# Loading q four tokens to a row, in the order in which the transposes write it, in a fused retention and bilinear feed-forward kernel

## The chip, the cores and the metric

The kernel runs on one core of a Trainium2 chip. The metric is the time of one execution on the device, in microseconds; the median of three runs counts. The traces come from the chip's own profiler.

## The reference

For 8 batches, 8 heads, 576 tokens and a head dimension of 64, a retention layer without softmax is computed, and its result goes through a bilinear feed-forward layer:

```python
scores = scale * np.matmul(q, k.transpose(0, 1, 3, 2))        # scale = 1/sqrt(64)
gamma = 1.0 - 2.0 ** (-5.0 - np.arange(H))                     # one decay a head
rel = pos[:, None] - pos[None, :]
Dmat = np.where(rel >= 0, gamma[:, None, None] ** rel[None], 0.0)
ret = np.matmul(scores * Dmat, v)                              # (8, 8, 576, 64)
x = ret.transpose(0, 2, 1, 3).reshape(4608, 512)
a, b = x @ w_a, x @ w_b                                        # 512 -> 1536
out = (a * b) @ w_out                                          # 1536 -> 512, float32
```

q, k, v and the weights are float32 in DRAM.

## The kernel before

All matrix products are in bfloat16 with float32 sums. The decay is split: values are scaled by gamma^-token, outputs by scale times gamma^token (the table `qs_o` in the opening), and between them stands a plain triangular mask. Tokens are handled in pairs of 128 rows (256 tokens); what lies more than a block back comes in through a running state (keys times values, summed).

**The opening.** The first 256 tokens of batches 0, 1 and 2 are handled in six steps, `STEPS = [(0, 0), (1, 0), (0, 1), (1, 1), (2, 0), (2, 1)]`: batch and half of the heads. Steps 0 to 3 (batches 0 and 1) are done before the feed-forward layer starts; steps 4 and 5 (batch 2) are done inside its first block. Here two tokens stand in a row: partition p holds tokens 2p and 2p+1, so that `load_step` (L152 to L163) moves pieces of 2 x 64 floats, 512 B, one DMA of 256 KB for each of q, k and v of a step. All go out on SP's queue, but K of step 0 on ACT's. Per step there are:

- `cast_step`: float32 to bfloat16, heads regrouped by token parity, one for q and one for k (DVE, POOL or ACT); `values_step`: the scaled values, in two parts
- `transpose_step`: four 128 x 128 transposes on TensorE for q and four for k, into one PSUM tile `tp`, and copies from there to `qkT` (L338)
- `score_step`: sixteen small products into `sc` (two PSUM banks, one tile for all steps) and the mask product on DVE into `sT` (L360)
- `state_step` and its parts: products of keys and values (L379), and copies of the state by ACT
- `open_step`, `step_states`, `step_keys`, `close_step`: output products from states (L449) and scores (L465), scaled on DVE into `xT` (L481, L486)

`warm` (L923) puts products of ones in between, whose results nobody reads. The order of the opening is written out by hand (L929 to L998): the order of the calls is the order on every engine's queue. `load_w` puts the weight loads, which turn float32 into bfloat16 on the way, on POOL's queue between casts; `load_wo` follows. After the opening, `gate`, a tiny copy out of `wo_sb`, holds SP's queue until the first piece of `w_out` has landed; behind it stand the loads of steps 4 and 5 and of the following pairs.

**The feed-forward layer.** It runs in blocks of 512 or 256 tokens: products `pa` (L860, in the first block partly L811 through `ffn_begin` and `begin_with`) and `pb` (L875), their product on DVE into `hT`, then `po` (L822 in the first block, else L896) and its copy to `osb`. The list `todo` holds the attention work that goes in between, each entry with a place in units of one 512-wide product: `early_casts` at 100, a q cast at 112.1, `third_turn` at 124, `third_states` at 128 and `third_outputs` at 136 are those of batch 2. The rest of the batches goes in pairs of 128 rows with one token a row (`load_pair`, `ahead`, `turn`, `stretch`), transposed by DMA instead of TensorE. `store` writes 128 rows of `osb`; for the first 256 tokens of batches 0 to 2 (`n < FIRST`) in two DMAs, one for each token parity. Stores of the first three blocks are held in `held` and sent from places in `todo`.

Four PSUM banks (`ps_ffn`, tag `ab`) rotate among `tp`, `w`, state products and the layer's products.

Of the kernel before, what the change touches and what calls it, by code (L numbers as in the profile page):

```python
# [10 lines left out]
FP32 = mybir.dt.float32  # L11
BF16 = mybir.dt.bfloat16
INT32 = mybir.dt.int32
# [5 lines left out]
def kernel(  # L19
# [10 lines left out]
    nc = tc.nc  # L30
# [123 lines left out]
    def load_step(n, hh, which, on=nc.sync):  # L154

        if n not in paired:
            paired[n] = [stage.tile([128, 2 * DM], FP32, tag=name, name=name)
                         for name in ("qf", "kf", "vf")]
        on.dma_start(
            paired[n][which][:, hh * DM:(hh + 1) * DM]  # L160
            .rearrange("p (h e) -> p h e", h=4),
            (q, k, v)[which][n, 4 * hh:4 * hh + 4, 0:256, :]
            .rearrange("h (p two) d -> p h (two d)", two=2))  # L163

    STEPS = [(0, 0), (1, 0), (0, 1), (1, 1), (2, 0), (2, 1)]
    Q, K, V = 0, 1, 2
    for i, which in ((0, Q), (0, K), (0, V), (2, Q), (2, K), (1, K),
                     (1, Q), (2, V), (3, K), (3, Q), (1, V), (3, V)):
        load_step(*STEPS[i], which,
                  nc.scalar if (i, which) == (0, K) else nc.sync)  # L170

# [1 line left out]

    idxp_i = const.tile([128, 2], INT32)
    nc.gpsimd.iota(idxp_i, pattern=[[1, 2]], base=0, channel_multiplier=2)
    idx_o = sum_pool.tile([128, 2, 2, 64], INT32, tag="sums", name="idx_o")
    nc.gpsimd.iota(idx_o, pattern=[[128, 2], [1, 2], [2, 64]], base=0,
                   channel_multiplier=0)
    identity = const.tile([128, 128], BF16)
    make_identity(nc, identity)  # L180
    mask_s = const.tile([128, 2, 2, 64], BF16)
    nc.gpsimd.memset(mask_s, 1.0)
    for a in (0, 1):
        nc.gpsimd.affine_select(
            out=mask_s[64 * a:64 * a + 64], in_=mask_s[64 * a:64 * a + 64],
            compare_op=ALU.is_ge, fill=0.0, base=0,
            pattern=[[-1, 2], [1, 2], [2, 64]], channel_multiplier=-2)
    idxv_i = const.tile([128, 3, 2], INT32)
    mask3 = const.tile([128, 64], BF16)

# [104 lines left out]

    QUADS = [(0, 0), (1, 1), (0, 1), (1, 0)]

    def place_step(i):
# [3 lines left out]
        transposed[key] = half_of(qkt_pool, i, [2, DM], BF16, "qkT")  # L302

    def given(i, which):
# [7 lines left out]
    COPY = {"dve": nc.vector.tensor_copy, "pool": nc.gpsimd.tensor_copy,  # L312
            "act": nc.scalar.copy}

    def cast_step(i, w, on):
        COPY[on](by_parity(natural[STEPS[i]][0][:, w]), given(i, w))  # L316

    def values_step(i, kp, on):
        n, hh = STEPS[i]
# [9 lines left out]
    def transpose_step(i, *ways):  # L329
        qkb, qkT = natural[STEPS[i]][0], transposed[STEPS[i]]  # L330
        tp = ps_ffn.tile([128, len(ways), 4, 128], BF16, tag="ab", name="tp")
        for to, (w, on) in enumerate(ways):
            for c in range(4):
                nc.tensor.transpose(tp[:, to, c, :],  # L334
                                    qkb[:, w, c * 128:c * 128 + 128],
                                    identity)
        for to, (w, on) in enumerate(ways):
            COPY[on](qkT[:, w], tp[:, to].rearrange("p c x -> p (c x)"))  # L338

    def queries(key, r, j, a):  # L340
        return transposed[key][r, 0].rearrange(
            "p (k j s) -> p j k s", k=2, j=2)[:, j, :, half(a)]

    def score_step(i, place=None, tag="sc"):
        key = STEPS[i]
# [54 lines left out]
        else:  # L400
            rest.append(keep)

    def last_states():

        own, later_half = kvs = [
            ps_ffn.tile([128, 2, 2, 64], FP32, tag="ab", name=f"kv1{a}")
            for a in (0, 1)]
        fresh = set(QUADS)
        for i in (1, 3):
            state_products(i, [kv[:, i // 2] for kv in kvs], fresh)  # L410
        for r in (0, 1):
            nc.scalar.copy(state_after[half(r), 1, :, half(r)],
                           own[half(r)].rearrange("p i j d -> p (i j) d"))
        nc.scalar.copy(own_sums[1],
                       own.rearrange("p i j d -> p (i j) d"))
        nc.scalar.copy(second[:, 1],
                       later_half.rearrange("p i j d -> p (i j) d"))
# [115 lines left out]
                decay[:, at], op=ALU.mult)  # L533
        natural[FIRST + n, "pair"] = (qkb, vb)

    def turn(n):
# [246 lines left out]
    def store(u, cols, osb):  # L783
        n, u = place(u // 2), u % 2
        for kp, r0, m, b, s0 in rows_of(n):
            rows = out[b * S + s0:b * S + s0 + m, cols]
            if kp != u:
                continue
            if n < FIRST:
                for par in (0, 1):  # L790
                    nc.sync.dma_start(rows[par::2], osb[half(par), cols])
            else:
                nc.sync.dma_start(rows, osb[r0:r0 + m, cols])

    held = []

# [130 lines left out]
    pieces = list(zip(edges, edges[1:]))  # L927
    vector, pool_ = nc.vector, nc.gpsimd
    warm(8, 512)  # L929
    make_qs(qs_o, 0, 0, 256)  # L930
    for i in range(4):
        place_step(i)
    cast_step(0, Q, "dve")
    cast_step(0, K, "dve")
    make_qs(qs_o, 1, 0, 256)
    transpose_step(0, (Q, "act"))
    transpose_step(0, (K, "dve"))
    values_step(0, 0, nc.scalar)
    values_step(0, 1, vector)
    make_qs(qs_o, 2, 0, 256)  # L940
    cast_step(2, Q, "pool")
    warm(2, 512)
    score_step(0)
    warm(1, 512)
    state_step(0)
    transpose_step(2, (Q, "dve"))
    cast_step(2, K, "pool")
    cast_step(1, K, "pool")
    warm(2, 512)
    transpose_step(2, (K, "dve"))  # L950
    warm(2, 512)
    load_w(*pieces[0], "a")
    cast_step(1, Q, "act")
    score_step(2)
    transpose_step(1, (K, "act"))
    output_step(0)
    transpose_step(1, (Q, "act"))
    values_step(2, 1, pool_)
    values_step(2, 0, pool_)
    make_qs(qs_o, 3, 0, 256)  # L960
    load_w(*pieces[0], "b")
    load_w(*pieces[1], "a")
    warm(2, 512)
    cast_step(3, K, "dve")
    score_step(1)
    cast_step(3, Q, "act")
    rest = []
    state_step(2, rest)
    warm(2, 512)
    transpose_step(3, (Q, "act"))  # L970
    transpose_step(3, (K, "dve"))
    rest.pop()()
    open_step(2)
    step_states(2, True)
    step_keys(2, {0})
    for kp in (0, 1):
        values_step(1, kp, pool_)
    values_step(3, 0, nc.scalar)
    values_step(3, 1, pool_)
    load_w(*pieces[1], "b")  # L980
    score_step(3)
    close_step(2)
    last_states()
    for i, banks in ((1, ps_ffn), (3, ps_sc)):
        open_step(i, banks)
        step_keys(i, {0, 1})
    for i in (1, 3):
        step_states(i, False)
    for i in (1, 3):
        close_step(i)  # L990
    firsts = ps_o[0].tile([128, 2, 512], FP32, tag="o", name="pa2")
    for F in range(WCOLS[0]):
        ffn_begin(F, firsts[:, F])
    for c in (0, 1):
        for F in range(WCOLS[0]):
            begin_with(F, c, 1)
# [3 lines left out]
        load_wo(i)  # L1000
    make_masks()
    nc.sync.dma_start(gate, wo_sb[0:1, 3, 0:64])
    for i, which in ((4, Q), (4, K), (4, V), (5, Q), (5, K), (5, V)):
        load_step(*STEPS[i], which)
    load_pair(FIRST)
    load_pair(FIRST + 1, (Q,))
# [14 lines left out]
    def early_casts():  # L1021
        for i in (4, 5):
            place_step(i)
        cast_step(4, Q, "act")
        for i in (4, 5):
            cast_step(i, K, "pool")
            for kp in (0, 1):
                values_step(i, kp, pool_)

# [30 lines left out]
    todo = [(100, early_casts, ()),  # L1060
            (112.1, cast_step, (5, Q, "act")),
            (124, third_turn, ()), (128, third_states, ()),
            (136, third_outputs, ())]
    todo += [(60 + 10 * n, total_of, (n,)) for n in (0, 1)]
# [31 lines left out]
    for fn, places in ((ahead, casts), (turn, turns)):  # L1096
        todo += [(at, fn, (n,)) for n, at in places.items()]
    todo.sort(key=lambda e: e[0])

# [41 lines left out]
```

## Time and profile before

| | |
|---|---|
| median of the runs (three) | 325.33 us (325.19 to 325.6) |
| the profiled execution | 325.76 us |
| its span in the profile | 324.0 us |
| busy: TensorE, VectorE (DVE) | 318.6 us, 165.5 us |
| busy: ScalarE (ACT), GpSimd (POOL) | 130.8 us, 118.8 us |
| DMA bytes | 50.90 MB, 157 GB/s in the mean |

The profile is that of one execution. PE is TensorE, SP the queue that issues most DMAs; a line number is one of the kernel before. The chain of waits follows the execution back from its last instruction, at each step to what released it. A DMA is given with the time from its issue to its landing, the moment at which its semaphore tells the waiting engines.

### The profile page before, as it was taken

The numbers are of one execution on the slowest core, as the hardware profiler recorded it, in microseconds if no ns is written. First come the engines' busy times: TensorE is split into PE (matmuls) and PEld (weight loads), VectorE is DVE, ScalarE is ACT, GpSimd is POOL, SyncE is SP. The second block draws the span as 40 slices with busy tenths as digits, with TensorE's granted clock in tenths as the row PEclk, the third lists the DMA queues.
The fourth block names the chain that finished last, engine by engine and source line by source line (L and its number), as shares of the span: only waits on it lengthen the run. The fifth ranks groups of instructions, "written<-read, shape, count | busy, mean of one in ns | idle before, by whom it ended". The sixth has DMA issues, their size and how long they took to land.

```text
span 324.0 us, 8659 instructions
## 1 busy us (share of the span) xinstructions
PE 318.6 (98%) x3607; PEld 164.4 (51%) x3607; DVE 165.5 (51%) x296; ACT 130.8 (40%) x289; POOL 118.8 (37%) x159
## 2 busy tenths in 40 slices
PE   8899999999999999999999999999999999999996
PEld 3554457777444554444454545454545444444444
DVE  4845345665546754835374627562566256514321
ACT  6745653435435523533253324442433343313321
POOL 3990076583745375457075205450520000000000
PEclk9999999999999999999999999999999999999999
DMA  8999999999999999999999168935750510031003
GB/s 215 253 202 207 261 229 195 197 181 197 182 223 243 218 192 240 229 223 230 182 211 195 47 156 194 214 78 144 169 113 15 141 42 2 2 97 32 1 23 109
DMA packets 146487, 50.90 MB, mean 157 GB/s; under 512 B 126736, under 2 KB 141968, under 8 KB 146448
## 3 DMA queue, kind: packets, MB, share of 16 engines
q1 hardware_dynamic: 140112, 45.37, 68.2%
q0 software_dynamic: 5808, 4.72, 9.3%
q8 instruction: 28, 0.46, 0.6%
q10 hardware_dynamic: 528, 0.26, 0.3%
q14 instruction: 11, 0.09, 0.1%
HBM read 37.75 MB, written 9.44 MB: 146 GB/s over the span
## 4 chain that ended last, share of the span: by engine, by line
PE 97%; ACT 1%; DVE 1%; issue 0%; DVEq 0%
PE pb L875 29%; PE pa L860 28%; PE po L896 28%; PE w L923 2%; PE po L822 2%; PE sc L635 2%; PE o L663 1%; PE o L676 1%; PE kv L573 1%; PE tp L334 1%; PE sc L352 1%; PE pa L811 1%; PE o L465 0%; ACT qkT L338 0%; ACT vb L324 0%
## 5 line engine op out<-in xcount | busy, mean ns | idle before, releaser
L880 DVE TENSOR_TENSOR hT<-ha,pb 128x512 bf16<-128x512 bf16 (+1 forms) x120 | 75.7, 632 | 93.7 <-PE pb L875 86.2
L875 PE MATMUL pb<-xT,wb_sb 128*128 128x512 bf16 (+1 forms) x480 | 111.6, 358 | 0.1
L868 ACT CAST ha<-pa 128x512 bf16<-128x512 f32 (+1 forms) x120 | 64.8, 543 | 113.6 <-PE pa L860 110.7
L860 PE MATMUL pa<-xT,wa_sb 128*128 128x512 bf16 (+1 forms) x472 | 109.8, 357 | 0.0
L896 PE MATMUL po<-wo_sb,hT 128*128 128x512 bf16 (+2 forms) x432 | 91.8, 367 | 0.0
L875 PEld LDWEIGHTS <-wb_sb 128*128 128x128 bf16 x480 | 46.9, 98 | 46.6 <-issue 0.3
L860 PEld LDWEIGHTS <-wa_sb 128*128 128x128 bf16 x472 | 45.4, 98 | 45.1 <-issue 0.4
L896 PEld LDWEIGHTS <-hT 128*128 128x128 bf16 x432 | 40.4, 98 | 44.4
L519 POOL CAST qkb<-qf 64x1024 bf16<-64x1024 f32 x15 | 15.4, 1030 | 68.2 <-DMA qf<-in_q_dram 57.9
L530 POOL TENSOR_TENSOR vb<-vf,vs 128x1024 bf16<-128x1024 f32 (+1 forms) x17 | 28.8, 1699 | 15.4 <-DMA vf<-in_v_dram 6.4
L907 DVE COPY osb<-po 128x512 f32<-128x512 f32 (+2 forms) x16 | 10.4, 649 | 39.1 <-PE po L896 39.1
L905 ACT COPY osb<-po 128x512 f32<-128x512 f32 (+1 forms) x20 | 11.4, 572 | 46.4 <-PE po L896 46.4
L519 POOL CAST qkb<-kf 64x1024 bf16<-64x1024 f32 (+1 forms) x17 | 15.9, 933 | 12.4 <-DMA kf<-in_k_dram 12.0
L598 DVE TENSOR_TENSOR sums<-kv,sums 128x256 f32<-128x256 f32 x44 | 18.6, 423 | 2.7 <-PE kv L573 0.8
L644 DVE TENSOR_TENSOR sT<-sc,mask 128x512 bf16<-128x512 f32 x30 | 19.5, 680 | 0.0
L523 POOL CAST qkb<-kf 64x512 bf16<-64x512 f32 (+1 forms) x34 | 18.6, 573 | 1.0
L523 POOL CAST qkb<-qf 64x512 bf16<-64x512 f32 x30 | 17.6, 614 | 0.6
L602 ACT CAST states<-sums 64x512 bf16<-64x512 f32 x26 | 16.0, 617 | 0.3
L689 DVE TENSOR_TENSOR xT<-o,qs 128x512 bf16<-128x512 f32 x24 | 15.4, 680 | 1.5 <-PE o L676 1.5
L923 PE MATMUL w<-ones 128*128 128x512 bf16 x19 | 7.4, 512 | 1.5 <-DVE idxp_f L204 1.5
L316 POOL CAST qkb<-kf 128x512 bf16<-128x512 f32 x4 | 2.4, 612 | 15.8 <-DMA kf<-in_k_dram 15.8
L360 DVE TENSOR_TENSOR sT<-sc,mask_s 128x1024 bf16<-128x1024 f32 x6 | 7.2, 1219 | 1.9 <-PE sc L352 1.8
(96 smaller groups left out, 173.4 us busy)
## 6 DMA issues: line engine op xcount, KB each, us to landing
qf<-in_q_dram SPq DMA_DIRECT2D x32, 256.0 KB, 4.8
vf<-in_v_dram SPq DMA_DIRECT2D x32, 256.0 KB, 5.1
kf<-in_k_dram SPq DMA_DIRECT2D x31, 256.0 KB, 4.8
out_dram<-osb SPq DMA_DIRECT2D x25, 256.0 KB, 2.5
out_dram<-osb SPq DMA_DIRECT2D x21, 128.0 KB, 2.7
wo_sb<-in_moe_w_out_dram POOLq DMA_DIRECT2D x3, 512.0 KB, 15.9
qf<-in_q_dram SPq DMA_DIRECT2D x8, 128.0 KB, 3.2
kf<-in_k_dram SPq DMA_DIRECT2D x8, 128.0 KB, 3.3
```

The source lines that it names most:

```text
L519: nc.gpsimd.tensor_copy(qkb[0:64, w, e], t[0:64, e])
L523: nc.gpsimd.tensor_copy(to[:, :, 1 - r], fro[:, :, r])
L530: nc.gpsimd.tensor_tensor(vb[:, e].rearrange("p (h d) -> p h d", d=D), t[:, e].rearrange("p (h d) -> p h d", d=D), decay[:, at], op=ALU.mult)
L598: nc.vector.tensor_tensor(sums[:, i], own, prev, op=ALU.add)
L602: nc.scalar.copy(to(half(1 - r)), fro(half(r)))
L644: nc.vector.tensor_tensor(sT[:, on].rearrange("p c k s -> p (c k) s"), sc[:, on].rearrange("p c k s -> p (c k) s"), mask3.unsqueeze(1).to_ ...
L689: nc.vector.tensor_tensor(x_of(t0, 128).rearrange("p c (a s) -> p c a s", a=2), o[:, :, :, kp].rearrange("p a c s -> p c a s"), qs[:, :, s ...
L860: nc.tensor.matmul(pa[:, 0:n], wa_sb[:, c, fs], xT[:, c], start=(c == 0), stop=(c == NC - 1))
L868: nc.scalar.copy(ha[:, 0:n], pa[:, 0:n])
L875: nc.tensor.matmul(pb[:, 0:n], wb_sb[:, c, fs], xT[:, c], start=(c == 0), stop=(c == NC - 1))
L880: nc.vector.tensor_tensor(hT[:, F, 0:n], has[F][:, 0:n], pb[:, 0:n], op=ALU.mult)
L896: nc.tensor.matmul(po[:, 0:width], hT[:, F, u * 128:(u + 1) * 128], wo_sb[:, F, cols], start=(F == 0), stop=(F == NF - 1))
```

## The change

For the three batches of the opening, q is no longer loaded by step but by batch, in four DMAs of 128 KB. DMA `h` takes heads `h` and `h + 4` to the two halves of the partitions, and each partition holds four tokens of one head, 1,024 B in one piece. The cast goes by pairs of DMAs (`cast_queries`), four transposes then turn two such pairs of heads (`turn_queries`), and `queries` reads 32 columns from each of four tokens' blocks. Keys and values stay as they were, two tokens a row. The query tokens so stand in another order in the mask, in `qs_o`, in `xT` and in the output rows, and `store` writes its 128 rows in one DMA whose DRAM side is walked as four groups of 32 rows.

The opening's order is written anew: other engines for several casts, copies and values (both value parts of step 0 on POOL, one part of step 3 on DVE), q of a batch turned at once, the kept state copies later, each `tp` tile holding four transposes rather than up to eight, two fillers fewer, and the first products of the layer (`ffn_begin`) ahead of the last products from the states instead of behind them.

```diff
@@ load_step
+        if which == Q:
+            for h in range(4):
+                on.dma_start(
+                    paired[n][Q][:, 256 * h:256 * h + 256],
+                    q[n, h::4, 0:256, :]
+                    .rearrange("g (p four) d -> g p (four d)", four=4))
+            return
@@ order of the loads
-    for i, which in ((0, Q), (0, K), (0, V), (2, Q), (2, K), (1, K),
-                     (1, Q), (2, V), (3, K), (3, Q), (1, V), (3, V)):
+    for i, which in ((0, Q), (0, K), (0, V), (2, K), (1, Q), (1, K),
+                     (2, V), (3, K), (1, V), (3, V)):
@@ casts, turns, queries
+    def cast_queries(n, j, on):
+        COPY[on](heads_q[n][:, j].rearrange("p (k h d) -> p h k d", h=2, k=4),
+                 paired[n][Q][:, j * DM:(j + 1) * DM]
+                 .rearrange("p (h k d) -> p h k d", h=2, k=4))
+    def turn(blocks, to, on):
+        tp = ps_ffn.tile([128, 4, 128], BF16, tag="ab", name="tp")
+        for c in range(4):
+            nc.tensor.transpose(tp[:, c, :], blocks[:, c * 128:c * 128 + 128],
+                                identity)
+        COPY[on](to, tp.rearrange("p c x -> p (c x)"))
+    def turn_queries(n, on):
+        for j in (0, 1):
+            turn(heads_q[n][:, j], turned_q[n][:, j], on[j])
     def queries(key, r, j, a):
-        return transposed[key][r, 0].rearrange(
-            "p (k j s) -> p j k s", k=2, j=2)[:, j, :, half(a)]
+        n, hh = key
+        p0 = 64 * hh + 32 * a
+        return turned_q[n][r, j].rearrange(
+            "p (k x) -> p k x", k=4)[:, :, p0:p0 + 32]
@@ store
             if n < FIRST:
-                for par in (0, 1):
-                    nc.sync.dma_start(rows[par::2], osb[half(par), cols])
-            else:
-                nc.sync.dma_start(rows, osb[r0:r0 + m, cols])
+                rows = rows.rearrange("(s k) m -> k s m", k=4)
+            nc.sync.dma_start(rows, osb[r0:r0 + m, cols])
@@ the opening, as it now stands
     warm(8, 512)
     for c in range(3):
         make_qs(qs_o, c, 0, 256)
     ...
     cast_keys(0, "dve")
     cast_queries(0, 0, "dve")
     cast_queries(0, 1, "act")
     turn_keys(0, "dve")
     turn_queries(0, ("act", "dve"))
     values_step(0, 0, pool_)
     values_step(0, 1, pool_)
     make_qs(qs_o, 3, 0, 256)
     cast_keys(2, "pool")
     warm(2, 512)
     score_step(0)
     warm(1, 512)
     state_step(0, keeps)
     turn_keys(2, "act")
     cast_queries(1, 0, "pool")
     load_w(*pieces[0], "a")
     cast_queries(1, 1, "act")
     warm(2, 512)
     score_step(2)
     keeps.pop()()
     cast_keys(1, "pool")
     open_step(0)
     step_states(0, True)
     step_keys(0, {0})
     warm(2, 512)
     turn_queries(1, ("act", "act"))
     turn_keys(1, "dve")
     close_step(0)
     values_step(2, 0, pool_)
     values_step(2, 1, pool_)
     load_w(*pieces[0], "b")
     warm(2, 512)
     score_step(1)
     cast_keys(3, "act")
     state_step(2, keeps)
     turn_keys(3, "act")
     open_step(2)
     step_states(2, True)
     step_keys(2, {0})
     values_step(1, 0, pool_)
     load_w(*pieces[1], "a")
     values_step(1, 1, nc.scalar)
     keeps.pop()()
     values_step(3, 0, vector)
     values_step(3, 1, pool_)
     load_w(*pieces[1], "b")
     score_step(3)
     close_step(2)
     ...
     for i, banks in ((1, ps_ffn), (3, ps_sc)):
         state_products(i, [kv[:, i // 2] for kv in kvs], fresh)
         open_step(i, banks)
         step_keys(i, {0, 1})
     last_copies(kvs)
     ...
     for F in range(WCOLS[0]):
         ffn_begin(F, firsts[:, F])
     for i in (1, 3):
         step_states(i, False)
     for i in (1, 3):
         close_step(i)
@@ batch 2, inside the first block
-    for i, which in ((4, Q), (4, K), (4, V), (5, Q), (5, K), (5, V)):
+    for i, which in ((4, Q), (4, K), (4, V), (5, K), (5, V)):
         load_step(*STEPS[i], which)
     def third_turn():
+        turn_queries(2, ("act", "act"))
         for i in (4, 5):
-            transpose_step(i, (Q, "act"), (K, "dve"))
+            turn_keys(i, "dve")
```

More of the change, by code (lines that the diff above doesn't have):

```diff
@@ L175 @@
     nc.gpsimd.iota(idxp_i, pattern=[[1, 2]], base=0, channel_multiplier=2)
-    idx_o = sum_pool.tile([128, 2, 2, 64], INT32, tag="sums", name="idx_o")
-    nc.gpsimd.iota(idx_o, pattern=[[128, 2], [1, 2], [2, 64]], base=0,
+    idx_o = sum_pool.tile([128, 2, 4, 32], INT32, tag="sums", name="idx_o")
+    nc.gpsimd.iota(idx_o, pattern=[[128, 2], [1, 4], [4, 32]], base=0,
                    channel_multiplier=0)
@@ L180 @@
     make_identity(nc, identity)
-    mask_s = const.tile([128, 2, 2, 64], BF16)
+    mask_s = const.tile([128, 2, 4, 32], BF16)
     nc.gpsimd.memset(mask_s, 1.0)
@@ L186 @@
             compare_op=ALU.is_ge, fill=0.0, base=0,
-            pattern=[[-1, 2], [1, 2], [2, 64]], channel_multiplier=-2)
+            pattern=[[-1, 2], [1, 4], [4, 32]], channel_multiplier=-2)
     idxv_i = const.tile([128, 3, 2], INT32)
@@ L296 @@
     QUADS = [(0, 0), (1, 1), (0, 1), (1, 0)]
+    heads_q, turned_q = {}, {}
     def place_step(i):
@@ L302, in place_step @@
         transposed[key] = half_of(qkt_pool, i, [2, DM], BF16, "qkT")
+        if i % 2 == 0:
+            heads_q[i // 2] = shared["qkb"][:, :, Q]
+            turned_q[i // 2] = shared["qkT"][:, :, Q]
     def given(i, which):
@@ L313, with cast_keys @@
             "act": nc.scalar.copy}
-    def cast_step(i, w, on):
-        COPY[on](by_parity(natural[STEPS[i]][0][:, w]), given(i, w))
+    def cast_keys(i, on):
+        COPY[on](by_parity(natural[STEPS[i]][0][:, K]), given(i, K))
+    def cast_queries(n, j, on):
+        COPY[on](heads_q[n][:, j].rearrange("p (k h d) -> p h k d", h=2, k=4),
+                 paired[n][Q][:, j * DM:(j + 1) * DM]
+                 .rearrange("p (h k d) -> p h k d", h=2, k=4))
     def values_step(i, kp, on):
@@ L327, in values_step, with turn_keys @@
                              .to_broadcast([128, 4, D]), op=ALU.mult)
[L329 to L338, printed above, removed]
+    def turn(blocks, to, on):
[4 more added lines that the diff above has]
+        COPY[on](to, tp.rearrange("p c x -> p (c x)"))
+    def turn_keys(i, on):
+        turn(natural[STEPS[i]][0][:, K], transposed[STEPS[i]][:, K], on)
+    def turn_queries(n, on):
+        for j in (0, 1):
+            turn(heads_q[n][:, j], turned_q[n][:, j], on[j])
     def queries(key, r, j, a):
-        return transposed[key][r, 0].rearrange(
-            "p (k j s) -> p j k s", k=2, j=2)[:, j, :, half(a)]
+        n, hh = key
+        p0 = 64 * hh + 32 * a
+        return turned_q[n][r, j].rearrange(
+            "p (k x) -> p k x", k=4)[:, :, p0:p0 + 32]
     def score_step(i, place=None, tag="sc"):
@@ L401, in state_copies, with last_copies @@
             rest.append(keep)
[L403 to L410, printed above, removed]
+    def last_copies(kvs):
+        own, later_half = kvs
         for r in (0, 1):
@@ L534, in ahead, with turn_pair @@
         natural[FIRST + n, "pair"] = (qkb, vb)
-    def turn(n):
+    def turn_pair(n):
         qkb = of(natural, n)[0]
@@ L929 @@
     warm(8, 512)
-    make_qs(qs_o, 0, 0, 256)
+    for c in range(3):
+        make_qs(qs_o, c, 0, 256)
     for i in range(4):
         place_step(i)
[L933 to L941, printed above, removed]
+    cast_keys(0, "dve")
+    cast_queries(0, 0, "dve")
+    cast_queries(0, 1, "act")
+    turn_keys(0, "dve")
+    turn_queries(0, ("act", "dve"))
+    values_step(0, 0, pool_)
+    values_step(0, 1, pool_)
+    make_qs(qs_o, 3, 0, 256)
+    cast_keys(2, "pool")
     warm(2, 512)
@@ L944 @@
     warm(1, 512)
[L945 to L948, printed above, removed]
-    warm(2, 512)
-    transpose_step(2, (K, "dve"))
-    warm(2, 512)
[L952 to L957, printed above, removed]
+    keeps = []
+    state_step(0, keeps)
+    turn_keys(2, "act")
+    cast_queries(1, 0, "pool")
+    load_w(*pieces[0], "a")
+    cast_queries(1, 1, "act")
+    warm(2, 512)
+    score_step(2)
+    keeps.pop()()
+    cast_keys(1, "pool")
+    open_step(0)
+    step_states(0, True)
+    step_keys(0, {0})
+    warm(2, 512)
+    turn_queries(1, ("act", "act"))
+    turn_keys(1, "dve")
+    close_step(0)
+    values_step(2, 0, pool_)
     values_step(2, 1, pool_)
-    values_step(2, 0, pool_)
-    make_qs(qs_o, 3, 0, 256)
     load_w(*pieces[0], "b")
-    load_w(*pieces[1], "a")
     warm(2, 512)
-    cast_step(3, K, "dve")
     score_step(1)
[L966 to L972, printed above, removed]
+    cast_keys(3, "act")
+    state_step(2, keeps)
+    turn_keys(3, "act")
     open_step(2)
@@ L975 @@
     step_keys(2, {0})
-    for kp in (0, 1):
-        values_step(1, kp, pool_)
-    values_step(3, 0, nc.scalar)
+    values_step(1, 0, pool_)
+    load_w(*pieces[1], "a")
+    values_step(1, 1, nc.scalar)
+    keeps.pop()()
+    values_step(3, 0, vector)
     values_step(3, 1, pool_)
@@ L982 @@
     close_step(2)
-    last_states()
+    kvs = [ps_ffn.tile([128, 2, 2, 64], FP32, tag="ab", name=f"kv1{a}")
+           for a in (0, 1)]
+    fresh = set(QUADS)
     for i, banks in ((1, ps_ffn), (3, ps_sc)):
+        state_products(i, [kv[:, i // 2] for kv in kvs], fresh)
         open_step(i, banks)
         step_keys(i, {0, 1})
+    last_copies(kvs)
+    firsts = ps_o[0].tile([128, 2, 512], FP32, tag="o", name="pa2")
+    for F in range(WCOLS[0]):
+        ffn_begin(F, firsts[:, F])
     for i in (1, 3):
@@ L990 @@
         close_step(i)
-    firsts = ps_o[0].tile([128, 2, 512], FP32, tag="o", name="pa2")
-    for F in range(WCOLS[0]):
-        ffn_begin(F, firsts[:, F])
     for c in (0, 1):
@@ L1023, in early_casts @@
             place_step(i)
-        cast_step(4, Q, "act")
+        cast_queries(2, 0, "act")
         for i in (4, 5):
-            cast_step(i, K, "pool")
+            cast_keys(i, "pool")
             for kp in (0, 1):
@@ L1056, in third_turn @@
     def third_turn():
+        turn_queries(2, ("act", "act"))
         for i in (4, 5):
[L1058 removed]
+            turn_keys(i, "dve")
     todo = [(100, early_casts, ()),
[L1061 removed]
+            (112.1, cast_queries, (2, 1, "act")),
             (124, third_turn, ()), (128, third_states, ()),
@@ L1095 @@
         casts[n], turns[n] = placed[n] - 70, placed[n] - 38
-    for fn, places in ((ahead, casts), (turn, turns)):
+    for fn, places in ((ahead, casts), (turn_pair, turns)):
         todo += [(at, fn, (n,)) for n, at in places.items()]
```

## The prediction

> **What bounds the kernel now.** I read the page first (shares of the engines, slices), then the chain of waits in order of time for the first 45 us, then the DMA view of the first 40 us and the DMA queue's own timeline.
>
> ```profile
> PE   8899999999999999999999999999999999999996
> DMA  8999999999999999999999168935750510031003
> PE 97%; ACT 1%; DVE 1%; issue 0%; DVEq 0%
> ```
>
> TensorE is busy in all slices and carries 97% of the chain. After the opening no matmul waits, so what the change is worth lies in the opening (until block 0's first `pb` product) and in the third batch's turn inside block 0. The DMA engines are just as full up to slice 22.
>
> ```profile
> 12.15 0.41 PE sc L352 x14
> ...
> 14.51 0.96 ACT vb L324 x4
> ...
> 16.14 0.55 PE o L465 x25
> 16.69 0.33 PE o L449 x4
> 17.02 1.75 PE pa L811 x16
> 18.77 1.73 PE pb L875 x8
> ...
> 42.94 0.86 PE po L896 x4
> 43.80 0.89 PE tp L334 x16
> ```
>
> This is the chain in order of time. The opening ends at 18.77, where `pb` starts. Filler products (`w` L923) and waits for ACT lie in it, so TensorE is not what is short there: the values of batch 1 (`vb` L324, 14.51) are among the last things to come. From 18.77 to 43.80, where the third batch is turned, TensorE runs without a gap: 25.0 us.
>
> ```profile
> GB/s 0 11 168 344 318 289 291 289 291 290 289 291 279 218 187 198 195 196 204 208 198 202 204 204 207 205 207 209 205 206 205 207 207 204 211 205 288 329 323 291
> q0 software_dynamic: 5808, 4.72, 75.1%
> q1 hardware_dynamic: 8126, 4.03, 38.8%
> q10 hardware_dynamic: 528, 0.26, 2.2%
> ```
>
> These are slices of 1 us and queues of the first 40 us. The opening's twelve copies of 256 KB run at 291 GB/s, 262144 B / 291 = 0.90 us each, and the weights follow without a pause. Queue q10 carried one copy alone (K of step 0, on ACT's queue): 528 packets are its 512 rows of 512 B and 16 more, one closing packet for each of 16 engines. The 2.2% of 16 x 40 us over 528 is 27 ns a packet.
>
> ```profile
> DMA packets 148, 0.13 MB, mean 222 GB/s; under 512 B 16, under 2 KB 148, under 8 KB 148
> q1 hardware_dynamic: 148, 0.13, 66.5%
> ```
>
> That is the window 321.1 to 321.7, where the last stores run in packets of mostly 1 KB: 66.5% of 16 x 0.6 us is 6.4 us, over 132 packets (without the closings) 48 ns. With 27 ns at 512 B I take 46 ns for a packet of 1 KB.
>
> **The q copies.** Two copies of 256 KB in 512 B pieces become four of 128 KB in 128 pieces of 1 KB. If all 16 engines carry one, it lasts 8 x 46 ns = 0.37 us, 0.74 for what took 0.90. The form speaks against that. The SBUF side is 128 x 256, but the DRAM side is walked as 2 x 64 x 256 (head pair, row, four tokens), and the program built from the change keeps that outermost 2; it can't be merged with the 64, since heads lie four apart. Every copy of before has an outermost count of 128 or 64 on both sides; even `gate`, 64 adjacent numbers, is carried as 16 x 4. A copy that is cut along its outermost count on both sides falls into two shares: 64 x 46 ns = 2.94 us on two engines while fourteen have nothing to do. The bounds are 0.37 us (16 engines) and 128 x 46 ns = 5.9 us (one engine). I take 2.94, since it is what the carried counts give.
>
> The Trainium skill, "DMA: Bandwidth & Descriptors", section "Why a DMA increments its semaphore by 16 and not by 1", has this as a rule: the engines used are the largest number up to 16 that divides the slowest dimension's size on both sides, which here gives two, and always the lowest-numbered. The 16 closings above agree for a count of 128; no run so far shows a smaller count.
>
> **Opening, on an engine that carries q.** Packets start at 1.9. The queue keeps its order, so the sum is: batch 0's q 11.8 and K of step 0 0.9 (to 14.6), V0 and K2 1.8 (16.4), batch 1's q 11.8 (28.2), the first weight piece in between 1.4 (256 KB at some 195 GB/s; 29.6), then K1, V2, K3, V1, V3 at 0.9 (34.1), landing 0.65 later, 34.8. Before, the last V landed at 14.0: K3 is issued at 5.81 and lands 5.5 us on, at 11.3, and three copies of 0.9 follow. The SP issues, now 17 instead of 11 at 0.5 us, hide behind the 2.94 of each q copy; without that cover the six cost 3 us.
>
> Behind V3 stand, in DVE's order, `values_step(3, 0)` (0.41) and then the mask product of step 3 (1.22): 34.8 to 36.4. The new end costs 3.2 us from there: keys 0.4, `ffn_begin` 0.9, states 0.3, then the closings of steps 1 and 3, which now wait for those states (0.44 + 0.68), and the last four products 0.4. Before, it was 18.77 - 15.99 = 2.8 (the mask product ends at 14.76 + 1.23). So `pb` starts at 39.6, 20.8 us later. The weights: `wb` piece 0 is issued on POOL behind values of step 2 (V2 lands at 31.8, plus 1.2), so at 33.0; with its 5.7 us to landing it is there at 38.7, just in time, and the others keep their distance.
>
> Casts, transposes, copies and score products are the same in number and size (casts 0.43 on DVE, 0.61 on ACT and POOL; turns 0.33; copies 0.42 to 0.59); where they move, they lie beside the waits for q and cost nothing. Without that cover their moves are worth -0.3 to +0.5: `close_step(0)` behind the copy of step 1's keys delays the next mask product by 0.3. Two filler products fewer: nothing.
>
> **Clock.** The first eight fillers take 3.59 us, 0.45 each; later 512-wide products take 2.59 / 12 = 0.22. Full rate came some 6 us after the start. Now TensorE stands still for many microseconds before 39.6. If that brings the slow start back, up to 6 us run at half rate, 3 us lost; if not, 0. Part falls into waits, so I take 1 here and 2 at the turn.
>
> The Trainium skill, "TensorE: Matmul & The Clock Gate", Part 1, says that an idle window of about 3.4 us returns the array to half clock and that about as much work lifts it; by that alone each place costs an estimated 1.7 us or more. No trace here shows a second slow start.
>
> **Third batch.** `gate` holds SP until the first `wo` piece has landed, 32.85 before; with weights 22.4 later that is 55.2. The q copies go out from 55.9, packets from 57.0, 11.8 us of them and 3 us of `wo` on the same two engines: q lands at 72.4, and K, V, K, V 0.9 apart until 76.0. TensorE reaches the turn at 43.80 + 21.8 = 65.6 and stops. POOL casts K of step 5 behind values of step 4 (73.3 + 0.6, then 74.2 + 1.2 + 0.6): 76.0; its turn ends at 76.3 instead of 44.7, so 31.6 later, 9.8 of them new. ACT stands in its queue behind the q cast too, with the `osb` copy already done. The pairs that follow stand behind those copies, which are about 32.5 late: the key transposes of pair 4 land at 63.4 for scores at 65.4, so 2 us of slack cover the missing 1.
>
> **Stores.** Six stores of 2 x 64 rows become one each of 4 x 32 rows: by the same cut 32 x 83 ns = 2.7 us on four engines. They go out from 95 to 126 us; TensorE waits for none. I take 0; if loads between them lose their slack, 2 to 4 us. Six SP issues of 0.6 fewer are hidden too.
>
> **Sum.** 20.8 + 1 + 9.8 + 2 = 33.6. The profiled execution took 325.76 (span 324.0, the rest around it), so 359.4; the median shown is 325.33, so 358.9.
>
> **Rivals.** (a) Sixteen engines carry each q copy. For it: all copies of before do. Then four times 0.16 us of stream go, V3 lands 0.6 earlier, and if the end's order costs nothing the opening ends 0.6 sooner: 324.7, faster. It decides from the point where a q copy posts 16 closings and V3 is there by 13.4. Against: the carried 2. Chance 0.05. (b) The same spread, but the closings that now wait for the states take the place (+0.4, and 0.3 from `close_step(0)`, less 0.2): 325.8, chance 0.04, mostly no change by measurement. (c) Two engines, and the weights become the bound too, since POOL issues them behind casts that wait for q, and each piece comes 2 to 4 us after its use; with stores that steal slack: 367. Chance 0.1. (d) One engine: twice 11.8 more in the opening and 11.8 in the third batch, 394; chance 0.02. The forecast keeps 0.79.
>
> **Numbers.** About 0.2%, 0.65 us, can be told from no change. Inside the forecast a packet of 44 to 56 ns moves 768 packets by -1.5 to +7.7 us, the clock by -3 to +3, slack by +4. If batch 1's q is partly hidden or the turn's wait is 4 us shorter, 347 to 350. Range 347 to 371, which takes in (c). Faster 0.05, same 0.03, slower 0.92.
>
> **What would show it.** q copies with a few closings and landings 2 to 3 us apart; ACT, POOL and DVE waiting on DMA `qf` for over 10 us; low GB/s until 30 us; `pb` first near 40; a stop at the turn of batch 2 near 66. If q lands before 7 us, the forecast is wrong altogether.

## The result and the profile after

| | before | after |
|---|---|---|
| median of the runs (six each) | 325.29 us (325.19 to 325.6) | 368.77 us (365.74 to 369.34) |
| ratio, 95% interval | | 1.1323 [1.1285, 1.1361] |
| profiled execution (span) | 325.76 us (324.0) | 369.34 us (367.6) |

The changed kernel is slower by 43.5 us; 358.9 had been forecast, in a range of 347 to 371, so the time is 9.9 us over the forecast and inside the range. Its page, in 40 slices of 9.2 us:

```profile
PE   4346999299999999879769999999999999999996
PEclk9986999779999999999969999999999999999999
DMA  1356995799999957896999993699286050012004
DMA packets 144711, 50.90 MB, mean 138 GB/s; under 512 B 126496, under 2 KB 140192, under 8 KB 144672
PE 70%; DMA 13%; SPq 11%; POOL 3%; DVE 1%; issue 1%; DVEq 0%; POOLq 0%
```

TensorE has three holes: slices 0 to 3 (until 37 us), slice 7 (64 to 74) and a shallower stretch from slice 16 to 20 (147 to 193), and the granted clock (PEclk, the share of its full clock that TensorE was given) falls to 0.6 or 0.7 in or behind each of them. The chain, 97% TensorE before, has 24% of DMA and of SP's queue. The packets under 512 B were 126,736 before and are 240 fewer: 288 closing packets (the one that each engine sends at the end of its share) are gone, six q copies and twelve stores with 16 each, and 48 have come, which is twelve copies with two and six with four.

The chain in order of time (start, duration, what), from its start to the end of the second hole:

```profile
3.80 3.06 SPq L161
...
16.58 3.15 SPq L161
...
22.49 8.52 DMA vf<-in_v_dram
31.15 1.19 POOL vb L343 x2
32.33 0.75 POOL wb_sb L273
...
38.78 15.44 DMA wo_sb<-in_moe_w_out_dram
54.24 0.65 SPq L1021
...
64.29 7.29 DMA vf<-in_v_dram
...
77.19 2.73 PE po L911 x8
...
80.72 1.83 PE po L911 x8
```

SP's own issues (`SPq`) now lead the chain: a load that took 0.5 us to issue before is held for 2.6 to 3.2. Not every one is: of the first four q issues the first two took 0.73 and 0.55, the next 1.58 and 3.06. A value tile lands at 31.0, the first `wo` piece at 54.2, which releases `gate` (L1021), and the next late value tile at 71.6. The DMA view of the first 40 us has slices of 1 us:

```profile
DMA  0081111111657111111111167799992111998989
GB/s 0 8 248 47 44 40 48 48 48 48 199 158 241 47 44 43 45 47 47 47 47 63 47 199 195 138 222 245 326 294 77 43 31 7 134 145 81 137 116 155
```

From 3 to 10 and from 13 to 23 us one tenth of the engines' time is in use, and 47 GB/s flow where 291 did. 131072 B / 47 is 2.79 us a q copy, by this rate 43.6 ns a packet on each of two engines. TensorE's timeline (in brackets the idle time before, and its releaser) shows the end of the first hole, with what led to it, and both ends of the second:

```profile
30.92 0.61 PE L349 MATMUL tp<-identity,qkb 128*128 128x128 bf16 x4 [1.44 <-POOL qkb L328]
...
34.55 0.42 PE L374 MATMUL sc<-qkT 64*64 64x128 bf16 x16
...
39.60 1.89 PE L890 MATMUL pb<-xT,wb_sb 128*128 128x512 bf16 x8
...
64.98 0.40 PE L349 MATMUL tp<-identity,qkb 128*128 128x128 bf16 x4 [0.18 <-ACT qkb L331]
70.73 1.36 PE L349 MATMUL tp<-identity,qkb 128*128 128x128 bf16 x8 [5.35 <-ACT qkb L331]
```

`pb` starts at 39.60, batch 2's turn stops at 65.4. In the windows of 4 us, the last three columns are granted clock, DMA share and GB/s:

```profile
24.00:28.00 4.00, 0.00 (x0) 0.00 (x0) 0.00 (x0) 0.00 (x0) 0.00 (x0) 0.55 1.02 200
28.00:32.00 4.00, 1.67 (x10) 0.98 (x10) 0.43 (x2) 2.20 (x6) 1.46 (x3) 0.50 0.66 185
...
72.00:76.00 4.00, 2.64 (x21) 1.17 (x24) 0.85 (x2) 0.00 (x0) 3.19 (x6) 0.50 0.83 188
```

The third stretch is TensorE waiting for transposes that a DMA makes (`qkT<-qkb`):

```profile
186.76 0.64 PE L652 MATMUL sc<-qkT 64*64 64x64 bf16 x32 [5.09 <-DMA qkT<-qkb]
```

Two more such waits stand at 149.34 (1.67 us) and 165.54 (2.68 us). Behind the last one the granted clock is 0.74 in the mean from 180 to 190 us. In the kernel before, TensorE waited for no `qkT`.

Where does the time come in? I set ACT's copies of `pa` (`ha`) beside the same copies of before, one by one. The first is 21.0 us late, from the second block on they are 31.7 late, those between 157 and 201 us go from 33.3 to 43.5 late, and from there to the end the distance stays at 43.6. So there are three costs: opening 21.0, turn of batch 2 10.7, and 11.8 between 120 and 200 us, of which the three waits are 9.4.

### The profile page after: what moved, and what is told of

Read it like the earlier page. It is cut to its first block, busy times and chain, and to the rows that moved or that the text cites. A ratio compares the mean times of both kernels' runs of the same rounds, so it can differ in the third digit from the quotient of the medians.

```text
span 367.6 us, 8648 instructions
## 1 busy us (share of the span) xinstructions
PE 328.1 (89%) x3605; PEld 168.3 (46%) x3605; DVE 165.2 (45%) x294; ACT 130.9 (36%) x287; POOL 119.7 (33%) x160
## 3 DMA queue, kind: packets, MB, share of 16 engines
q0 software_dynamic: 5808, 4.72, 8.5%
## 4 chain that ended last, share of the span: by engine, by line
PE 70%; DMA 13%; SPq 11%; POOL 3%; DVE 1%; issue 1%; DVEq 0%; POOLq 0%
PE po L911 23%; PE pa L875 21%; PE pb L890 21%; SPq L161 6%; DMA vf<-in_v_dram 4%; DMA wo_sb<-in_moe_w_out_dram 4%; SPq L166 3%; DMA kf<-in_k_dram 2%; DMA qkT<-qkb 2%; PE sc L652 1%; PE o L693 1%; PE o L680 1%; SPq L148 1%; POOL vb L343 1%; SPq L808 1%; PE kv L590 1%
## 5 line engine op out<-in xcount | busy, mean ns | idle before, releaser
L911 PE MATMUL po<-wo_sb,hT 128*128 128x512 bf16 (+2 forms) x432 | 95.5, 378 | 0.0
L911 PEld LDWEIGHTS <-hT 128*128 128x128 bf16 x432 | 41.4, 100 | 46.8 <-issue 4.3
L920 ACT COPY osb<-po 128x512 f32<-128x512 f32 (+1 forms) x20 | 11.4, 570 | 55.2 <-PE po L911 55.2
L349 PE MATMUL tp<-identity,qkb 128*128 128x128 bf16 x48 | 6.9, 293 | 24.7 <-ACT qkb L331 10.8
L540 POOL CAST qkb<-kf 64x512 bf16<-64x512 f32 (+1 forms) x34 | 18.7, 576 | 1.0
L349 PEld LDWEIGHTS <-qkb 128*128 128x128 bf16 x48 | 4.1, 126 | 28.0 <-ACT qkb L331 17.2
L652 PE MATMUL sc<-qkT 64*64 64x64 bf16 x480 | 7.3, 198 | 9.4 <-DMA qkT<-qkb 9.4
```

Of the source, the lines that this page charges most:

```text
L540: nc.gpsimd.tensor_copy(to[:, :, 1 - r], fro[:, :, r])
L911: nc.tensor.matmul(po[:, 0:width], hT[:, F, u * 128:(u + 1) * 128], wo_sb[:, F, cols], start=(F == 0), stop=(F == NF - 1))
```

## The experiments

Differences in us are against the runs of the kernel before on the same chip, whose median lay between 325.35 and 325.81.

**Stores and q apart.** The first three kernels repair one part, the other and both. A store by row is four copies of 32 plain rows; a q copy by row is walked with the row outermost (64 x 2 x 256 on the DRAM side, 128 partitions on the other), so that `queries` picks its columns with a step of two.

```diff
@@ e1_stores_by_row, against after
             if n < FIRST:
-                rows = rows.rearrange("(s k) m -> k s m", k=4)
-            nc.sync.dma_start(rows, osb[r0:r0 + m, cols])
+                for k4 in range(4):
+                    nc.sync.dma_start(rows[k4::4],
+                                      osb[32 * k4:32 * k4 + 32, cols])
+            else:
+                nc.sync.dma_start(rows, osb[r0:r0 + m, cols])
@@ e2_q_by_row, against after
-                    .rearrange("g (p four) d -> g p (four d)", four=4))
+                    .rearrange("g (p four) d -> p g (four d)", four=4))
...
-            "p (k x) -> p k x", k=4)[:, :, p0:p0 + 32]
+            "p (k x) -> p k x", k=4)[:, :, 64 * a + hh:64 * a + 64:2]
@@ e3_both_by_row: both edits
```

> The changed kernel, but each store of the first 256 tokens goes out as four copies of 32 rows, whose outermost count is 32, instead of one copy walked as 4 x 32 rows. Theory (a copy is cut along its outermost count, so the one store runs on four engines and holds up the loads behind it there): of the 43.5 us lost, 11.8 lie between 120 and 190 us, where scores wait for transposes; they go, and the time falls from 368.8 to some 357, with those waits of 9.4 us gone. Rival (these waits come from the lateness of batch 2's loads and would be there whatever the stores do): 367 to 369.

> The changed kernel, but the four q copies of a batch are walked row first (64 x 2 x 256 instead of 2 x 64 x 256 on the DRAM side; partition 2p + g instead of 64 g + p, and the scores and states read every second column). Same bytes, same 128 pieces of 1,024 B, same number and order of copies; the stores stay walked as 4 x 32. Theory (two engines carried each q copy): q of both batches lands before 10 us, the opening ends at 18 to 20 instead of 39.6, the turn of batch 2 no longer waits, and the time falls by 28 to 32 us, to 326 to 341, according to what the stores still cost. Rival (the smaller and more numerous copies, SP's issues of 0.5 to 3 us each, or the new order of the opening make it late): the opening still ends after 30 us and the time stays above 355.

> The changed kernel with both repairs: q copies walked row first and stores as four copies of 32 rows. It shows what the rest of the change is worth (1 KB pieces, the opening's new order, four transposes a tile). Theory: 1 KB pieces take 46 ns instead of twice 27, so the stream of q, k and v is 0.6 us shorter, and the end of the opening costs 0.4 us more: 324.5 to 326.0, within 0.7 us of before. Rival (the new order is what costs): over 328.

| | stores 4 x 32 in one | stores by row |
|---|---|---|
| q 2 x 64 | after: 368.77, +43.5 | e1: 357.45 (356.81 to 358.4), +31.8; 1.0975 [1.0951, 1.0999] |
| q by row | e2: 343.05 (341.37 to 344.12), +17.4; 1.0527 [1.0498, 1.0555] | e3: 328.78 (328.57 to 332.54), +3.1; 1.0121 [1.0085, 1.0157] |

The form of the stores costs 11.7 us beside the spread q and 14.3 beside the repaired one; the form of q costs 26.1 and 28.7. In e1 the `ha` copies are 21.1 late after the opening and 31.6 from the second block to the end: the third cost is gone, and TensorE's waits for `qkT` with it. e2 missed its range of 326 to 341 by 2 us and is far from its rival's (above 355). SP's queue shows what the stores do. First after, then e1, the same list of issues (start, duration, what; xN issues):

```profile
125.38 0.69 SPq L808 DMA_DIRECT2D out_dram<-osb  x1
...
128.63 4.30 SPq L808 DMA_DIRECT2D out_dram<-osb  x1
...
135.16 4.62 SPq L808 DMA_DIRECT2D out_dram<-osb  x1
139.89 6.51 SPq L559 DMA_TRANSPOSE qkT<-qkb  x2
...
158.62 4.93 SPq L559 DMA_TRANSPOSE qkT<-qkb  x2
```

```profile
126.14 2.48 SPq L808 DMA_DIRECT2D out_dram<-osb  x4
...
136.26 2.64 SPq L559 DMA_TRANSPOSE qkT<-qkb  x2
...
148.80 4.97 SPq L559 DMA_TRANSPOSE qkT<-qkb  x2
```

Two of the six stores hold SP for over 4 us where four copies of 32 rows take 2.5 together. Others went out in 0.69 and 1.04, and then what stands behind is held: two V loads took 5.10 behind the fourth (at 151.64; 1.96 in e1). Behind the first three stores the transposes go out 3.6 us late, behind the fourth 9.8 (158.62 against 148.80). e3 came out above what was expected of it (324.5 to 326.0) and in the range of its rival, that the new order costs: the rest of the change is not free.

**The stores without the rest.** The kernel before, with each of its two-parity stores in one DMA walked as 2 x 64 rows.

```diff
@@ e8_before_store2, against before
             if n < FIRST:
-                for par in (0, 1):
-                    nc.sync.dma_start(rows[par::2], osb[half(par), cols])
-            else:
-                nc.sync.dma_start(rows, osb[r0:r0 + m, cols])
+                rows = rows.rearrange("(s k) m -> k s m", k=2)
+            nc.sync.dma_start(rows, osb[r0:r0 + m, cols])
```

> The kernel before, with one part of the change alone: each store of the first 256 tokens goes out as one copy walked as 2 x 64 rows (its two token parities) instead of two copies of 64 rows. Theory (cut along the outermost count: two engines, 64 packets of 84 ns, 5.4 us a store, 32 us in six stores; with four engines 16 us of such work cost 14.3): nearly all of it shows, 345 to 356. Rival (a walked store costs SP a fixed time, whatever the number of engines): like four groups, 336 to 340. Second rival (with q on time the loads have slack): within 2 us of before.

344.52 us (343.59 to 345.51), +18.7; 1.0572 [1.0545, 1.0599]. That is half a microsecond under the range of the theory, and far above those of both rivals: neither four-group stores (336 to 340) nor slack (within 2 us) fit. Opening and turn are those of before within 0.7 us; the rest comes in after 95 us. The packets under 512 B are 180 fewer than before: six stores with two closings in place of twelve with 16. SP's queue of this kernel, and behind it a line of the kernel before:

```profile
97.47 4.81 SPq L148 DMA_DIRECT2D kf<-in_k_dram  x2
...
112.55 7.55 SPq L542 DMA_TRANSPOSE qkT<-qkb  x2
```

```profile
103.72 2.73 SPq L542 DMA_TRANSPOSE qkT<-qkb  x2
```

The hold falls on whatever stands behind the store, not on the store alone: two K loads took 1.31 in this place before (96.68), two transposes 2.73 (103.72).

**The stores on another queue.** POOL issues the six strided stores of e2.

```diff
@@ e10_store_on_pool, against e2
                 rows = rows.rearrange("(s k) m -> k s m", k=4)
-            nc.sync.dma_start(rows, osb[r0:r0 + m, cols])
+                nc.gpsimd.dma_start(rows, osb[r0:r0 + m, cols])
+            else:
+                nc.sync.dma_start(rows, osb[r0:r0 + m, cols])
```

> As the run with q walked row first and the stores still walked as 4 x 32 rows (343.1 us), but these six stores are issued on POOL's queue instead of SP's. Theory (SP's queue is held, 4.7 and 5.5 us at two of the stores, because a store's packets on few engines stand in the same rings as the loads): without them in SP's rings the loads share the four engines packet by packet, SP is held less, and a part of the 14.3 us goes: 333 to 340. Rival (only the four engines' time counts, whatever the queue): 342 to 345.

339.55 us (338.53 to 342.69), +14.0; 1.0415 [1.0392, 1.0439], at the upper edge of what was expected. Of the 14.3 us of the stores 3.4 come back; most of the price stays. The stores no longer stand in SP's queue, and yet its loads are held: two V loads took 7.37 us at 103.67, where before they took 2.28 (99.86). The profiled execution, the longest of the four (342.69), has one wait of 7.4 us for `qkT`; e2's has three, 9.7 together. That the stores and loads share engines would fit this, but is not shown: the edit changes more than the queue. Issued by POOL a store is 272 packets instead of 132 (queue q0 has 7,440 packets against 5,808 in e2, q1 137,712 against 138,504); how many engines carry these is not known, and how far POOL's own work behind the stores takes part was not tried.

**The turn alone.** e3, with batch 2's q walked as in the changed kernel.

```diff
@@ e11_q2_alone, against e3
-                    .rearrange("g (p four) d -> p g (four d)", four=4))
+                    .rearrange("g (p four) d -> g p (four d)" if n == 2 else
+                               "g (p four) d -> p g (four d)", four=4))
```

(`queries` follows it for this batch.)

> As the run with both repairs (328.8 us), but batch 2's four q copies alone are walked 2 x 64 x 256 again, as in the change; partitions 64 g + p for this batch. Theory (11.8 us of packets on two engines, with the K and V copies of batch 2 behind them): the turn of batch 2 waits as in the changed kernel, where this step cost 10.5 us: 338.0 to 340.5. Rival (that step was long because the opening before it was late): under 334.

338.81 us (338.55 to 339.92); 1.041 [1.039, 1.0429]. That is +13.2, 10.1 more than e3; in the changed kernel the step was 10.7. TensorE's timeline has the same stop, 19 us earlier:

```profile
52.09 0.61 PE L350 MATMUL tp<-identity,qkb 128*128 128x128 bf16 x4 [5.37 <-ACT qkb L332]
```

**Smaller copies on all engines.** e1, with each q copy cut into two of 64 partitions.

```diff
@@ e4_q_by_head, against after with e1's stores
+                for g in (0, 1):
+                    on.dma_start(
+                        paired[n][Q][64 * g:64 * g + 64,
+                                     256 * h:256 * h + 256],
+                        q[n, h + 4 * g, 0:256, :]
+                        .rearrange("(p four) d -> p (four d)", four=4))
```

> As the one with both repairs, but the partitions stay as in the change (64 g + p), and each q copy is cut into two of 64 partitions by hand: eight copies of 64 KB a batch, each with the outermost count 64, so on 16 engines. Theory: SP's issue of 0.5 us each now sets the start, eight of them 4 us before V and K can go, so q of batch 0 lands at about 7 instead of 5.5 us: 326 to 329. Rival (the interleaving of the partitions, not the engines, made the difference in the run with q walked row first): over 350.

336.41 us (335.85 to 339.55); 1.0347 [1.0311, 1.0384]. This misses the expectation, and the rival falls too. The spread is repaired, but SP takes 5.05 us for eight issues in a row, 0.63 each, and V of step 0 is issued at 5.89 instead of 3.49: 64 KB each 0.63 us is 104 GB/s. The loads are bound by their issue (124 GB/s from 4 to 8 us), and 7.6 us over e3 are the price. The packets under 512 B are 480 more than before, as 24 q copies and 24 stores with 16 closings each give.

**What is left: 3.1 us.** Five kernels looked for it. e3's opening has holes in TensorE's work, and a granted clock of 0.50 to 0.70 between 8 and 16 us in the profiled execution (which took 330.88, 2.1 above the median, so that steps of 1 us can't be read from it: e11 has the same opening, and there `pb` starts at 20.30 instead of 22.98). e5 fills the holes, e6 issues V of step 0 on ACT's queue, e7 does both and takes before's order of the last products, e9 is e6 with the first weight piece later.

```diff
@@ e5_fillers, against e3
-    warm(1, 512)
+    warm(5, 512)
...
-    warm(2, 512)
+    warm(4, 512)
@@ e6_v_on_act, against e3
-                  nc.scalar if (i, which) == (0, K) else nc.sync)
+                  nc.scalar if (i, which) in ((0, K), (0, V)) else nc.sync)
@@ e9_weights_later, against e6
-    load_w(*pieces[0], "a")
     cast_queries(1, 1, "act")
     ...
     cast_keys(1, "pool")
+    load_w(*pieces[0], "a")
```

> As the run with both repairs (328.8 us, opening 4.4 us longer than before), with six more filler products of 512 columns: five instead of one behind the scores of step 0, four instead of two ahead of those of step 2. In the repaired run the granted clock is 0.70 from 8 to 12 us and 0.50 from 12 to 16. Theory (TensorE stands still while values of step 0 and K of step 2 are late, and the half clock that follows costs about 1 us of the 4.4): the clock stays at 1.00 from 4 us on, 327.4 to 328.2. Rival (the half clock falls into waits for q, k and v anyway): 328.5 to 329.3.

> As the run with both repairs, but V of step 0 is issued on ACT's queue behind K of step 0, so that it doesn't stand behind four q issues of 0.6 us each on SP's. In the repaired run it lands at 7.97 us (5.92 before), POOL waits 5.0 us for it, and casts of K and q stand behind it on POOL. Theory (SP's issues set the opening's start, not the engines): V lands before 6.5, all that stands behind it on POOL comes 1 to 1.5 us earlier, and the time falls to 327.0 to 328.0. Rival (the copies of the opening are bound by bytes, so what one gains another loses): 328.4 to 329.2.

> As the run with both repairs, with the six fillers, with V of step 0 on ACT's queue, and with the end of the opening in the order of before (state products of steps 1 and 3 first, products from the states and closings ahead of ffn_begin). Theory (issues, clock and the end's order make up the 4.4 us): pb starts within 1 us of before's 18.8 and the time is 325.0 to 326.5. Rival (1 KB pieces don't pay, or POOL's longer list of values and casts binds): 327 or more.

> As the run with both repairs and V of step 0 on ACT's queue (329.5 us; in its profile the last V lands at 16.2, 3 us behind the V before it, while the first weight piece, issued at 8.9, lands at 16.1), but that weight piece is issued on POOL behind the cast of step 1's keys instead of ahead of it, some 1.5 us later. Theory (weights share the engines with the last V and make it late): the last V lands at 14.2 to 15, the opening ends 1 us sooner, 327.5 to 328.8. Rival (weights that come later are missed at pb, or the opening's new order is the bound): 329.2 to 331.

e5: 330.92 (1.0155 [1.0121, 1.0189]); e6: 329.54 (1.0124 [1.0099, 1.0148]); e7: 328.72 (1.01 [1.0077, 1.0123]); e9: 329.24 (1.0106 [1.0091, 1.0122]). The first three miss (e7 falls in its rival's range, 327 or more), e9 tells nothing apart: all intervals overlap that of e3. With the fillers of e5 the granted clock is 1.00 from 4 to 16 us, but it falls later, at the end of the opening (the third last column):

```profile
20.00:24.00 4.00, 3.69 (x32) 2.60 (x32) 1.91 (x4) 1.14 (x4) 4.00 (x7) 0.50 1.05 127
```

So e5 moved the half clock and did not show what it costs. The single executions say more. In e3 the four with a mean granted clock of 0.999 or 1.000 took 328.57 to 328.80 us, the two with 0.990 took 330.88 and 332.54. A stretch at half clock so goes with 2 us and more, but the 3.1 us of the median are there without it. V of step 0 on ACT's queue lands at 4.93 instead of 7.97, but the last V comes at 16.23 then (14.82 in e3).

The last kernel asks it from the other side: the kernel before, with the loads of q cut to 128 KB and in the changed order, nothing else.

```diff
@@ e12_before_loads, against before
+        if which == Q:
+            for g in (0, 2):
+                on.dma_start(
+                    paired[n][Q][:, hh * DM + 128 * g:hh * DM + 128 * g + 256]
+                    .rearrange("p (h e) -> p h e", h=2),
+                    q[n, 4 * hh + g:4 * hh + g + 2, 0:256, :]
+                    .rearrange("h (p two) d -> p h (two d)", two=2))
+            return
...
-    for i, which in ((0, Q), (0, K), (0, V), (2, Q), (2, K), (1, K),
-                     (1, Q), (2, V), (3, K), (3, Q), (1, V), (3, V)):
+    for i, which in ((0, Q), (2, Q), (0, K), (0, V), (2, K), (1, Q), (3, Q),
+                     (1, K), (2, V), (3, K), (1, V), (3, V)):
```

> This is the kernel before with nothing changed but the loads of q in the opening: each 256 KB copy of a step's q is cut into two of 128 KB (two heads each, two tokens a row, 512 B pieces, all 16 engines), and the order of the loads is that of the changed kernel, the whole q of a batch ahead of V of step 0 and K1 behind the second batch's q. It asks where the 3.1 us lie by which the repaired kernel (q and stores by row) stays above the kernel before. Theory: the loads. SP issues 15 copies instead of 11 at 0.5 to 0.6 us, the early stream is underfed (249 GB/s instead of 297 between 4 and 8 us), V of step 0 lands some 2 us later, and that moves the values, the states and all behind them: 327.2 to 329.5. Rival: the loads are hidden, and it is the new order of casts, turns and copies on DVE, POOL and ACT that costs: 325.0 to 326.2. In between, both have a part.

327.19 us (326.94 to 328.01), +1.8; 1.0054 [1.0041, 1.0068]: at the lower edge of the theory and outside the rival's range. The windows from 4 to 8 us of before, e12 and e3, in this order (last column GB/s):

```profile
4.00:8.00 4.00, 4.00 (x46) 1.74 (x44) 1.93 (x5) 2.50 (x7) 0.83 (x2) 1.00 1.17 297
```

```profile
4.00:8.00 4.00, 2.99 (x30) 1.17 (x29) 1.19 (x3) 1.02 (x2) 0.61 (x1) 1.00 0.98 274
```

```profile
4.00:8.00 4.00, 3.51 (x34) 1.76 (x33) 1.59 (x5) 2.49 (x5) 0.00 (x0) 1.00 0.85 249
```

So the changed loads cost 1.8 us in the kernel before, with its own order of work; that they cost as much of the 3.1 is argued from this. The early stream is underfed in e12 as in e3; by how much differs from execution to execution (e2 and e11, with e3's opening, have 268 and 280 in this window). Cutting and order weren't tried apart. The rest, 1.3 by the medians (2.2 with an uncertainty of 1.2 by the ratios), stays open: the longer issue of 1 KB pieces (four in 2.64 us in e3, 2.00 in e12) and the new order of casts, turns and copies are both left. None of the repaired versions came under the kernel before.

## Why the prediction was right or wrong

- **Two engines for a q copy, four for a store: right.** 240 closings fewer fit two and four, and a q copy took 2.79 us by the rate instead of the 2.94 forecast. The Trainium skill, "DMA: Bandwidth & Descriptors", "Why a DMA increments its semaphore by 16 and not by 1", had the engines as the largest number up to 16 that divides the slowest dimension on both sides; the trace agrees for 2 and for 4. e2 and e3 confirm it by the opposite: with 64 rows outermost, the same 128 KB in the same 1 KB pieces no longer flow at 47 GB/s, and the packets under 512 B come out as 16 closings a copy give them (126,664 in e2 and 127,024 in e3; 126,736 before).
- **Opening: right in size and cause; that it fits to 0.1 us is luck.** Forecast 20.8 and 1 for the clock; measured 21.0, with `pb` at 39.60 where 39.6 stood (40.6 with the clock). Values of step 2 were to land at 31.8 and came at 31.0; the `gate` was put at 55.2 and opened at 54.2. The last wait was another than forecast: not V of step 3 (its scaling on DVE began at 34.15, without a wait for it) but K of step 1, cast at 30.25. Behind it TensorE ran without a stop from 30.92, and the mask product of step 3 waited for the scores at 34.55 until 35.04; it ended at 36.27, where 36.4 stood.
- **Third batch: right, with its parts shifted.** Forecast 9.8 and 2, measured 10.7 (e11 alone: 10.1). The last turn ended at 74.1, not 76.3, 29.4 us later than before, so 8.4 were new by then: the `gate` opened 1.0 earlier, and too much was put beside q on the two engines. The other 2.3 came behind the turn, where 2 had been put for the clock: the granted clock was 0.50, and `po` took 0.34 us a product (2.73 / 8) until about 80 us, then 0.23.
- **Clock: the second slow start exists.** The forecast left it between 0 and 3 us at each place. By the Trainium skill, "TensorE: Matmul & The Clock Gate", Part 1, an idle window of about 3.4 us returns the array to half clock; the trace agrees, with 0.50 to 0.59 behind the stop of 5.35 us. In the opening the clock was 0.50 too until 34 us, in part while TensorE ran without a stop and others waited for it; what this adds to the 21.0 was not separated.
- **Stores: the term that was mis-sized.** Taken as 0, at most 2 to 4; measured 11.7 (e1) to 14.3 (e3 against e2), 18.7 in the kernel before with two engines (e8). The step that failed is "TensorE waits for none". It looked at who waits for the stores, and not at what stands behind them in SP's order: K, V and q loads and the transposes of the next pairs. The holds of 4.3 to 6.5 us add up, until the transposes go out 9.8 us later than in e1 and the slack is used up. Its 11.8, less the 1.9 by which opening and turn were put too high, are the 9.9 us by which the forecast was short.
- **"Without that cover their moves are worth -0.3 to +0.5": open.** With the spread repaired, 3.1 us stay (e3), which hold the moves and the issues together. The forecast had said that the added issues would cost 3 us once the slow q copies no longer cover them; e12 bears out 1.8 of that, and the moves are in the rest, 1.3 by the medians.
- **Rival (c), 367, had the right time by a part of the right reason.** Its stores did steal slack; but its weights did not become the bound: `pb` started where the forecast had it, and TensorE waited for no weights behind it. The range was drawn to take in (c), so that it holds the time is owed in part to a sum that was not the one forecast. Rivals (a), (b) and (d) fall by the 240 closings and by `pb` at 39.60.

## What to carry to other kernels

Read the carried form of a copy before its size: what is outermost on both sides decided how many engines worked here, and an outermost 2 took the stream of loads from 291 to 47 GB/s. Price such a copy not only by who waits for it but by the queue that it holds: what is issued behind it is late too, and holds add up until slack is gone. Larger pieces gained nothing here, where more copies of 0.5 to 0.6 us each had to be issued.

## What the runs showed of the hardware

- SP's issues are held when copies that few engines carry pile up: up to 3.2 us for a q copy on two engines and 4.3 to 4.6 for two of the stores on four, against 0.5 to 0.6 for a copy on all; the first of a row go out at once (0.73 and 0.55; 0.69 for the first store). The hold also falls on ordinary loads and transposes behind them (7.55 us for two transposes in e8, 2.73 before).
- Moving those stores to POOL's queue, which changed their packets too, gave back only 3.4 of 14.3 us, and loads on SP's queue were still held (7.37 us for two).
- An issue of 128 KB takes 0.47 us in 512 B pieces (e12) and 0.55 to 0.70 in 1 KB pieces (e3); 64 KB in 1 KB pieces takes 0.63 (e4). So the time of an issue did not follow the bytes.
- The granted clock shows 0.50 behind a stop of 5.35 us. At the start of an execution it can't be read as the speed: it shows 1.00 in the first microseconds of every kernel here, although the first fillers ran at half rate there. In the changed kernel two fillers at 16.32 took 1.06 us at a shown 1.00, as much as two at 31.32 at a shown 0.50; two at 21.40 took 0.60.
